# Block attention and feed-forward in one kernel: batch 0's scores from unsplit queries and keys

## The chip, the cores and the metric

The kernel runs on one core of a Trainium2 chip. The metric is the device time of one execution in microseconds, and a version's time is the median of its runs. The engines are called TensorE or PE (matmuls; PEld is its weight load), VectorE or DVE, ScalarE or ACT, GpSimd or POOL, and SyncE or SP, which here issues the DMAs.

## The reference

Inputs are float32: q, k and v of shape (8, 8, 576, 64) (batch, heads, sequence, head dimension) and two weight matrices, w_in (512 x 2048) and w_out (2048 x 512).

```python
scores = (1 / 8) * np.matmul(q, k.transpose(0, 1, 3, 2))
mask = pos[:, None] // 64 >= pos[None, :] // 64        # causal in blocks of 64
scores = np.where(mask, scores, -1e9)
attn = np.exp(scores - max(scores)); attn = attn / (sum(attn) + 1e-9)
x = np.matmul(attn, v)            # (B, H, S, D), then as rows: (B * S, H * D) = (4608, 512)
h = x @ w_in
g = h where h >= 1, 0 where h <= -1, (h + 1) ** 2 / 4 between
out = g @ w_out                   # (4608, 512)
```

## The kernel before

**Words.** The matmuls that need more than one rounded word keep their operands as two: a value is rounded to the type F32R (`hi`), and the remainder (`lo`) is a second F32R value. A product is then two or three matmuls that add up in PSUM. Plain F32 operands can be multiplied too, by one matmul instruction of the source.

**Attention.** There are 32 pairs: 8 batches of 4 pairs of heads, `Pair(b, hp)`. A pair's sequence of 576 is four tiles of 128 and a last block of 64; the last blocks of the two heads share one tile of 128. `SM` is 512, `S` 576, `D` 64 and `P` 128. For a pair, `load_qk` brings q and k in; `split_q` and `split_k` make the two words of each in the tiles `qs` and `ks` (VectorE, and GpSimd for the remainder of k, L353 to L366); `turned(is_q, j)` transposes head j's words on PE (L424), ScalarE copies both words out of PSUM into `qb` or `kb` (L429), and one word of them goes on to `qa` or `ka` by a DMA from SBUF to SBUF (L435; in the very first pair by VectorE for head 0, L431). `turned_last` does the same for the last blocks (L453, L458, L459, without a DMA). `qa` and `ka` hold one word of q and of k in partitions 0 to 63, and four rows more, 64 to 67 (`D` to `KA`), with which the product also adds the mask: the row set is made once in `mrow` at the start (L122 to L138) and copied there by DMA (L150, L151).

`scores(j, g)` makes the scores of head j for a group g of query tiles: group 0 holds tiles 0 and 1 (128 and 256 key columns), group 1 tile 2 (384), group 2 tile 3 (512). `scores_last` takes both heads' last blocks in two halves of 288 columns. Each score product is two matmuls:

```python
nc.tensor.matmul(ps, qa[:KA, j, c0 : c0 + P], ka[:KA, j, k0 : k0 + n], start=first, stop=False)   # L484
nc.tensor.matmul(ps, qb[:, j, c0 : c0 + P], kb[:, j, k0 : k0 + n], start=False, stop=last)        # L487
```

Then VectorE takes the maximum (L508, L533), ScalarE the exponential with its sum (L513, L539), VectorE the scaling (L519, L548). `turn` and `turn_last` transpose the result on PE (L559 or L561) and ScalarE copies it out (L552); `weighted` multiplies by v (L598); L633 and L634 round the result into `xh` and `xl`, the input of the second half.

Batches differ. In batches 0 and 1 (`plain`) the weighted sums are plain F32 matmuls. From batch 2 on (`raw`) q and k are copied first within HBM and split after the transposition.

**Feed-forward.** `ffn_in` (L777) and `ffn_out` (L801, L806) work on chunks of 512 tokens and 128 hidden columns, with two words each. The weights are split into words on the chip, in 32 pieces by `convert` (L165 to L188: a DMA load, ScalarE, VectorE, GpSimd). 

**Order.** A pair is written as eight steps. In the source's order, from step `START` = 36 on, one step of the feed-forward follows each step of attention; 12 of the 32 weight pieces, and two more for the lag, are started within the first 36 steps. The Tile framework orders each engine's instructions when the program is built, by that priority and by readiness, and engines work their queues in order. A tile's buffer is named by its pool and tag; a tag with one buffer gives it to the next tile only when all uses of the tile before are done. `qs` and `ks` have one buffer each, and their tags serve the `raw` batches too. `pa11` is used in batch 1 for a small piece. The loaded `qn` and `kn` share three buffers.

Of the kernel before, what the change touches and what calls it, by code (L numbers as in the profile page):

```python
# [8 lines left out]
F32 = mybir.dt.float32  # L9
# [14 lines left out]
def block_attn_then_ffn(  # L24
# [27 lines left out]
    SCALE = 1.0 / float(D) ** 0.5  # L52
# [4 lines left out]
    KA = D + NTL  # L57
# [2 lines left out]
    FAR = 2  # L60
    RAW = 2
    AT_HOME = 2

    const = ctx.enter_context(tc.tile_pool(name="const", bufs=1))
    att1 = ctx.enter_context(tc.tile_pool(name="att1", bufs=1))
# [12 lines left out]
    def work_bank(name):  # L78

        banks["n"] += 1  # L80
        if banks["free"] and banks["n"] % 2:
            return ps_o.tile([P, 512], F32, tag="po", name=name)
        return ps_w.tile([P, 512], F32, tag="work", name=name)
# [6 lines left out]
    ident = ident_r.bitcast(F32)  # L90
# [11 lines left out]
    qa = const.tile([P, 2, QW], F32R, tag="qa", name="qa")  # L102
    qb = const.tile([P, 2, QW], F32R, tag="qb", name="qb")
    ka = const.tile([P, 2, S], F32R, tag="ka", name="ka")
    kb = const.tile([P, 2, S], F32R, tag="kb", name="kb")

    def last_blocks(t_):

        view = t_[:, :, SM : SM + BLK]
        if t_.shape[2] == S:  # L110
            return view
        part, (_, two), cols = view.ap
        return bass.AP(tensor=view.tensor, offset=view.offset, ap=[part, [QW + BLK, two], cols])


    mrow = att1.tile([NTL, 2, S], F32R, tag="pb0", name="mrow")
# [5 lines left out]
    mtmp = ffn.tile([P, 512], F32, tag="t", name="mtmp")  # L122
# [13 lines left out]
    rows = mrow[:, :, :SM].rearrange("p s (t c) -> p s t c", c=P)  # L136
    nc.vector.tensor_copy(rows[:, 0, :, :BLK], sel)
    nc.vector.tensor_scalar_mul(rows[:, 1, :, BLK:], sel, MASKED)  # L138
    for t_ in (qa, qb):
        nc.vector.tensor_copy(  # L140
            t_[:, :, SM:], mtmp[:, : 2 * (QW - SM)].rearrange("p (h c) -> p h c", h=2)
        )
    for t_ in pcs:
        nc.vector.tensor_copy(t_[BLK:], mtmp[BLK:, : 2 * BLK].rearrange("p (h c) -> p h c", h=2))
    for t_ in vsr:
        nc.vector.tensor_copy(
            t_[BLK:, NTL, :, :], mtmp[BLK:, : 2 * D].rearrange("p (h c) -> p h c", h=2)
        )
    for j in range(2):
        nc.sync.dma_start(qa[D:KA, j, :S].bitcast(F32), mrow[:, 0, :].bitcast(F32))  # L150
        nc.sync.dma_start(ka[D:KA, j, :].bitcast(F32), mrow[:, 1, :].bitcast(F32))  # L151


    shifted = []
# [102 lines left out]
    class Pair:  # L257
# [4 lines left out]
        def __init__(self, b, hp):  # L262
            self.b, self.hp = b, hp

            self.plain = b < PLAIN
            self.first = b == 0 and hp == 0


            self.hop = b >= HOP
            self.raw = b >= RAW  # L270

            self.far = b >= FAR
            self.pr, self.nat = {}, {}

        def fetch(self):
# [68 lines left out]
            self.nat[name] = t_  # L344

        def split_q(self):
            if self.raw:
                return

            qn = self.nat.pop("q")[:, : 2 * NTL + 1, :]  # L350
            self.qs = att1.tile([P, 2 * NTL + 1, 2, D], F32R, tag="qs", name="qs")
            for c0, c1 in ((0, 2 * NTL), (2 * NTL, 2 * NTL + 1)):
                nc.vector.tensor_scalar_mul(self.qs[:, c0:c1, 0, :], qn[:, c0:c1, :], SCALE)  # L353
            nc.vector.scalar_tensor_tensor(
                out=self.qs[:, :, 1, :], in0=qn, scalar=SCALE,
                in1=self.qs[:, :, 0, :].bitcast(F32), op0=ALU.mult, op1=ALU.subtract,
            )

        def split_k(self):
            if self.raw:  # L360
                return
            kn = self.nat.pop("k")[:, : 2 * NTL + 1, :]
            self.ks = att1.tile([P, 2 * NTL + 1, 2, D], F32R, tag="ks", name="ks")
            for c0, c1 in ((0, 2 * NTL), (2 * NTL, 2 * NTL + 1)):
                nc.vector.tensor_copy(self.ks[:, c0:c1, 1, :], kn[:, c0:c1, :])
            (nc.vector if self.first else nc.gpsimd).tensor_tensor(  # L366
                out=self.ks[:, :, 0, :], in0=kn, in1=self.ks[:, :, 1, :].bitcast(F32),
                op=ALU.subtract,
            )
# [29 lines left out]
        def turned_raw(self, j):  # L399
# [10 lines left out]
            for a, bt, hi0 in ((qa, qb, 0), (ka, kb, D)):  # L410
                nc.sync.dma_start(
                    a[:D, j, :SM].bitcast(F32), bt[hi0 : hi0 + D, j, :SM].bitcast(F32)
                )

        def turned(self, is_q, j):

            if self.raw:
                if is_q:
                    self.turned_raw(j)
                return  # L420
            src, a, bt, hi0 = (self.qs, qa, qb, 0) if is_q else (self.ks, ka, kb, D)
            ps = work_bank("ps_qk")
            for t in range(NTL):
                nc.tensor.transpose(  # L424
                    ps[:, t * P : (t + 1) * P].bitcast(F32R), src[:, j * NTL + t, :, :], ident_r
                )

            turned = ps[:, :SM].rearrange("p (t c) -> p c t", t=NTL)
            nc.scalar.copy(bt[:, j, :SM].rearrange("p (c t) -> p c t", t=NTL), turned)  # L429
            if self.first and j == 0:  # L430
                nc.vector.tensor_copy(  # L431
                    a[:D, j, :SM].rearrange("p (c t) -> p c t", t=NTL), turned[hi0 : hi0 + D]
                )
            else:
                nc.sync.dma_start(  # L435
                    a[:D, j, :SM].bitcast(F32), bt[hi0 : hi0 + D, j, :SM].bitcast(F32)
                )

        def turned_last(self):

            ps = work_bank("ps_qk")
            if self.raw:
                ps = ps[:, :P]
                nc.tensor.transpose(ps.bitcast(F32R), self.qk[:, 2 * NTL, :, :], ident_r)
                ps = ps.rearrange("p (h c) -> p h c", h=2)
                self.parted(last_blocks, ps)
                for i, a in enumerate((qa, ka)):
                    nc.vector.tensor_scalar_mul(
                        last_blocks(a)[:D], ps[i * D : (i + 1) * D], 1.0 if i else SCALE
                    )  # L450
                return
            for i, src in enumerate((self.qs, self.ks)):
                nc.tensor.transpose(  # L453
                    ps[:, i * P : (i + 1) * P].bitcast(F32R), src[:, 2 * NTL, :, :], ident_r
                )
            for i, (a, bt, hi0) in enumerate(((qa, qb, 0), (ka, kb, D))):
                blocks = ps[:, i * P : (i + 1) * P].rearrange("p (h c) -> p h c", h=2)
                nc.scalar.copy(last_blocks(bt), blocks)  # L458
                nc.vector.tensor_copy(last_blocks(a)[:D], blocks[hi0 : hi0 + D])  # L459
# [21 lines left out]
                self.x32 = att1.tile([P, S], F32, tag="x32", name="x32")  # L481

        def product(self, ps, j, c0, k0, n, first, last):
            nc.tensor.matmul(  # L484
                ps, qa[:KA, j, c0 : c0 + P], ka[:KA, j, k0 : k0 + n], start=first, stop=False
            )
            nc.tensor.matmul(  # L487
                ps, qb[:, j, c0 : c0 + P], kb[:, j, k0 : k0 + n], start=False, stop=last
            )
# [7 lines left out]
        def scores(self, j, g):  # L497
# [9 lines left out]
            for i, cs in enumerate(cols):  # L507
                nc.vector.tensor_reduce(  # L508
                    out=nm[:, i : i + 1], in_=ps[:, cs], axis=AX.X, op=ALU.max, negate=True
                )  # L510
            raw = ps if self.b < AT_HOME else pr
            for i, cs in enumerate(cols):
# [379 lines left out]
```

## Time and profile before

| What | Value |
|---|---|
| median of 3 runs | 1239.24 us (1237.13 to 1243.8) |
| the profiled execution | 1239.06 us, its span 1237.3 us |
| granted TensorE clock, mean | 0.989 |
| instructions | 19822 |
| DMA | 215.40 MB, mean 174 GB/s |
| first score product (L484) starts | 13.69 us |
| last transposed weights of batch 0 (L561, second head) | about 103 us |

The span is the time from the first to the last instruction on the core. Busy shares are averages over stages that differ: the first 100 us hold batch 0's attention and almost no feed-forward, the last 200 us almost only feed-forward. In the timeline a row is: start, duration, engine, source line, operation, output and inputs, and in brackets the idle time ahead of it with what ended it. In a row of windows the columns are: window, length, then PE, PEld, DVE, ACT and POOL busy with the number of instructions, the granted clock, the DMA share and GB/s. In the chain of work a row is: start, length, engine and line.

### The profile page before, as it was taken

To read this page: it belongs to the slowest core of one execution; us is meant where nothing else is said; L and a number is where in the kernel's file an instruction comes from. 1 tells how busy PE (TensorE), PEld (TensorE's weight loads), DVE (VectorE), ACT (ScalarE), POOL (GpSimd) and SP (SyncE) were. 2 spreads that over 40 slices of the span, in tenths; PEclk is the share of its full clock that TensorE was granted. 3 is DMA by queue.
4 is the path that set the end of the run, shared out by engine and by line. 5 is a ranking of instruction groups with operands and counts; after the bars stand their busy time and mean duration, and the time that the engine had idled before them with its cause. 6 is when DMAs were issued, how large, how long until landed. Compare 5 with 4: busy or idle time off the path is not lost.

```text
span 1237.3 us, 19822 instructions
## 1 busy us (share of the span) xinstructions
PE 1186.6 (96%) x6280; PEld 993.1 (80%) x6280; DVE 863.8 (70%) x2124; ACT 698.5 (56%) x1731; POOL 371.8 (30%) x366
## 2 busy tenths in 40 slices
PE   4878898999999999999999999999999999999998
PEld 3666677788888888888888888888888888888886
DVE  8888778658777877787777877787778776322322
ACT  5877667546566656665666665666566654222222
POOL 3444546312222222222222222222222222222222
PEclk9988998999999999999999999999999999999999
DMA  5756776778986655565555555565556443333332
GB/s 165 213 176 208 235 247 221 225 202 255 291 270 219 192 162 156 147 198 166 163 159 180 164 160 160 148 196 151 155 149 192 142 135 111 119 102 102 120 103 102
DMA packets 177192, 215.40 MB, mean 174 GB/s; under 512 B 109872, under 2 KB 128304, under 8 KB 176320
## 3 DMA queue, kind: packets, MB, share of 16 engines
q1 hardware_dynamic: 177088, 214.14, 56.1%
q8 instruction: 50, 0.82, 0.3%
q14 instruction: 54, 0.44, 0.1%
HBM read 134.74 MB, written 31.98 MB: 135 GB/s over the span
## 4 chain that ended last, share of the span: by engine, by line
PE 86%; DVE 5%; DMA 4%; ACT 2%; issue 2%; POOL 1%; SPq 0%; ACTq 0%; DVEq 0%; POOLq 0%
PE ph L777 31%; PE po L801 20%; PE po L806 10%; PE ps_av L598 9%; PE ps_s L484 5%; PE ps_s L487 4%; PE ps_t L559 4%; PE ps_qk L403 1%; DMA bits<-in_moe_w_in_dram 1%; DVE bits L172 1%; POOL bits L184 1%; PE ps_t L561 1%; DVE nm L508 1%; DVE bits L178 1%; DVE shifted L175 1%
## 5 line engine op out<-in xcount | busy, mean ns | idle before, releaser
L792 POOL TENSOR_TENSOR gl<-t,gh 128x512 fp32r<-128x512 f32 x144 | 186.5, 1295 | 522.8 <-ACT gh L791 338.2
L801 PE MATMUL po<-wo,gh 128*128 128x512 f32 x1152 | 294.1, 396 | 0.1
L801 PEld LDWEIGHTS po<-wo,gh 128*128 128x128 f32 x1152 | 211.2, 188 | 43.3 <-ACT gh L791 0.6
L777 PE MATMUL ph<-xh,wih 128*128 128x512 f32 x576 | 232.7, 404 | 0.4 <-DVE t L790 0.4
L777 PE MATMUL ph<-xh,wil 128*128 128x512 f32 x576 | 228.1, 396 | 0.0
L777 PE MATMUL ph<-xl,wih 128*128 128x512 f32 x576 | 226.9, 394 | 0.0
L787 DVE SCALAR_TENSOR_TENSOR t<-t 128x512 f32<-128x512 f32 x144 | 101.0, 701 | 161.5 <-ACT t L786 158.6
L786 ACT ACTIVATE t<-ph 128x512 f32<-128x512 f32 x144 | 86.2, 599 | 160.5 <-PE ph L777 160.5
L791 ACT CAST gh<-t 128x512 fp32r<-128x512 f32 x144 | 89.4, 621 | 118.9 <-DVE t L790 118.8
L806 PE MATMUL po<-wo,gl 128*128 128x512 f32 x576 | 155.3, 391 | 0.0
L484 PE MATMUL ps_s<-ka,qa 68*128 68x288 f32 (+4 forms) x384 | 133.8, 363 | 4.9 <-DMA ka<-mrow 4.0
L513 ACT ACTIVATE pr<-ps_s,nm 128x128 f32<-128x128 f32 x192 | 100.4, 525 | 57.5 <-DVE nm L508 56.4
L508 DVE TENSOR_REDUCE nm<-ps_s 128x1 f32<-128x128 f32 (+3 forms) x256 | 118.9, 482 | 16.4 <-PE ps_s L487 15.6
L777 PEld LDWEIGHTS ph<-xh,wil 128*128 128x128 f32 x576 | 109.1, 189 | 24.0
L806 PEld LDWEIGHTS po<-wo,gl 128*128 128x128 f32 x576 | 108.0, 188 | 22.9
L777 PEld LDWEIGHTS ph<-xl,wih 128*128 128x128 f32 x576 | 109.6, 190 | 19.3
L777 PEld LDWEIGHTS ph<-xh,wih 128*128 128x128 f32 x576 | 109.2, 190 | 19.3 <-DVE t L790 0.8
L381 POOL TENSOR_TENSOR vsr<-vn,vsr 64x64 fp32r<-64x64 f32 (+1 forms) x96 | 56.5, 589 | 227.1 <-ACT vsr L380 226.0
L487 PE MATMUL ps_s<-kb,qb 128*128 128x288 f32 (+4 forms) x384 | 120.4, 321 | 0.0
L790 DVE TENSOR_TENSOR t<-ph,t 128x512 f32<-128x512 f32 x144 | 98.7, 685 | 2.0
L559 PEld LDWEIGHTS ps_t<-ident_r,prr 128*128 128x128 f32 x600 | 68.5, 139 | 22.4 <-issue 0.5
L494 DVE TENSOR_SCALAR sm<-sm 128x1 f32<-128x1 f32 x256 | 38.5, 151 | 65.0 <-ACT pr L513 54.8
(115 smaller groups left out, 1879.7 us busy)
## 6 DMA issues: line engine op xcount, KB each, us to landing
wo<-wo_split SPq DMA_DIRECT2D x144, 512.0 KB, 3.4
prr<-pr SPq DMA_DIRECT2D x96, 192.0 KB, 3.0
prr<-pr SPq DMA_DIRECT2D x48, 256.0 KB, 2.8
out_dram<-ob SPq DMA_DIRECT2D x36, 256.0 KB, 2.9
bits<-in_moe_w_in_dram SPq DMA_DIRECT2D x16, 512.0 KB, 4.6
bits<-in_moe_w_out_dram SPq DMA_DIRECT2D x16, 512.0 KB, 4.0
wo_split<-ws SPq DMA_DIRECT2D x16, 512.0 KB, 2.9
qa<-qb SPq DMA_DIRECT2D x63, 128.0 KB, 2.4
```

The costliest lines, as they stand in the source:

```text
L484: nc.tensor.matmul(ps, qa[:KA, j, c0 : c0 + P], ka[:KA, j, k0 : k0 + n], start=first, stop=False)
L487: nc.tensor.matmul(ps, qb[:, j, c0 : c0 + P], kb[:, j, k0 : k0 + n], start=False, stop=last)
L508: nc.vector.tensor_reduce(out=nm[:, i : i + 1], in_=ps[:, cs], axis=AX.X, op=ALU.max, negate=True)
L513: nc.scalar.activation(raw[:, cs], ps[:, cs], AF.Exp, bias=nm[:, i : i + 1], scale=1.0, accum_out=sm[:, i : i + 1],)
L559: nc.tensor.transpose(out.bitcast(F32R), src, ident_r)
L598: nc.tensor.matmul(ps[:, lo_col:], vt, x, start=first and i == 0 and m == 0, stop=last and i == len(parts) - 1 and m == len(mov) - 1,)
L777: nc.tensor.matmul(ph, w[:, cc, fs], x[:, cc, xs], start=(cc == 0 and i == 0), stop=(cc == NCC - 1 and i == 2),)
L787: nc.vector.scalar_tensor_tensor(out=t_, in0=t_, scalar=1.0, in1=t_, op0=ALU.min, op1=ALU.mult)
L790: nc.vector.tensor_tensor(out=t_, in0=ph, in1=t_, op=ALU.max)
L792: nc.gpsimd.tensor_tensor(out=gl, in0=t_, in1=gh.bitcast(F32), op=ALU.subtract)
L801: nc.tensor.matmul(po[tt], gh[:, ts_], wo[:, w, :], start=(fc == 0 and w == 0), stop=False)
L806: nc.tensor.matmul(po[tt], gl[:, ts_], wo[:, 0, :], start=False, stop=fc == NFC - 1)
```

## The change

In batch 0 (`WHOLE` = 1) q and k are not split. `turned_whole` transposes the loaded F32 tiles (64 columns wide instead of the 128 of two words), and ScalarE copies the result, with the scale for q, straight into `qw` or `kw`; there is no second copy by DMA. The last blocks of q go into a tile of their own, `ql`. A score product is one F32 matmul. `qw` and `kw` use the buffers of the tags `qs` and `ks`, `ql` that of `pa11`. The mask's rows are copied into `qw` and `kw` as well (four DMAs more, ahead of those into `qa` and `ka`), and `ql` is cleared at the start. Batches 1 to 7 are as before.

```diff
+    WHOLE = 1
...
+    qw = att1.tile([P, 2, SM], F32, tag="qs", name="qw")
+    ql = att1.tile([P, 2, P], F32, tag="pa11", name="ql")
+    kw = att1.tile([P, 2, S], F32, tag="ks", name="kw")
...
+    nc.vector.tensor_copy(ql, mtmp[:, : 2 * P].rearrange("p (h c) -> p h c", h=2))
...
-    for j in range(2):
-        nc.sync.dma_start(qa[D:KA, j, :S].bitcast(F32), mrow[:, 0, :].bitcast(F32))
-        nc.sync.dma_start(ka[D:KA, j, :].bitcast(F32), mrow[:, 1, :].bitcast(F32))
+    for a, b in ((qw, kw), (qa, ka)):
+        n = min(S, a.shape[2])
+        for j in range(2):
+            nc.sync.dma_start(a[D:KA, j, :n].bitcast(F32), mrow[:, 0, :n].bitcast(F32))
+            nc.sync.dma_start(b[D:KA, j, :].bitcast(F32), mrow[:, 1, :].bitcast(F32))
...
         def split_q(self):
-            if self.raw:
+            if self.raw or self.whole:
                 return
...
         def split_k(self):
-            if self.raw:
+            if self.raw or self.whole:
                 return
...
+        def turned_whole(self, is_q, j):
+
+            src, dst = (self.nat["q"], qw) if is_q else (self.nat["k"], kw)
+            ps = work_bank("ps_qk")[:D]
+            for t in range(NTL):
+                nc.tensor.transpose(ps[:, t * P : (t + 1) * P], src[:, j * NTL + t, :], ident)
+            nc.scalar.mul(
+                dst[:D, j, :SM].rearrange("p (c t) -> p c t", t=NTL),
+                ps[:, :SM].rearrange("p (t c) -> p c t", t=NTL),
+                SCALE if is_q else 1.0,
+            )
...
         def turned_last(self):
             ps = work_bank("ps_qk")
+            if self.whole:
+                for i, (name, dst) in enumerate((("q", ql), ("k", kw))):
+                    cols = ps[:D, i * P : (i + 1) * P]
+                    nc.tensor.transpose(cols, self.nat.pop(name)[:, 2 * NTL, :], ident)
+                    nc.scalar.mul(
+                        last_blocks(dst)[:D],
+                        cols.rearrange("p (h c) -> p h c", h=2),
+                        1.0 if i else SCALE,
+                    )
+                return
...
         def product(self, ps, j, c0, k0, n, first, last):
+            if self.whole:
+                tile_q = ql[:KA, j, :] if c0 == SM else qw[:KA, j, c0 : c0 + P]
+                nc.tensor.matmul(
+                    ps, tile_q, kw[:KA, j, k0 : k0 + n], start=first, stop=last
+                )
+                return
```

`last_blocks`, the view of a tile's last-block columns, is made general so that it fits `ql` and `kw` too.

More of the change, by code (lines that the diff above doesn't have):

```diff
@@ L105, in block_attn_then_ffn @@
     kb = const.tile([P, 2, S], F32R, tag="kb", name="kb")
+    qw = att1.tile([P, 2, SM], F32, tag="qs", name="qw")
+    ql = att1.tile([P, 2, P], F32, tag="pa11", name="ql")
+    kw = att1.tile([P, 2, S], F32, tag="ks", name="kw")
     def last_blocks(t_):
-        view = t_[:, :, SM : SM + BLK]
+        at = max(0, min(SM, t_.shape[2] - 2 * BLK))
+        view = t_[:, :, at : at + BLK]
         if t_.shape[2] == S:
-            return view
+            return t_[:, :, SM:]
         part, (_, two), cols = view.ap
-        return bass.AP(tensor=view.tensor, offset=view.offset, ap=[part, [QW + BLK, two], cols])
+        step = t_.shape[2] + BLK
+        return bass.AP(tensor=view.tensor, offset=view.offset, ap=[part, [step, two], cols])
     mrow = att1.tile([NTL, 2, S], F32R, tag="pb0", name="mrow")
@@ L272, in __init__ @@
             self.far = b >= FAR
+            self.whole = b < WHOLE
             self.pr, self.nat = {}, {}
@@ L413, in turned_raw @@
                 )
+        def turned_whole(self, is_q, j):
[8 more added lines that the diff above has]
+            )
         def turned(self, is_q, j):
+            if self.whole:
+                return self.turned_whole(is_q, j)
             if self.raw:
@@ L483, in product @@
         def product(self, ps, j, c0, k0, n, first, last):
+            if self.whole:
+                tile_q = ql[:KA, j, :] if c0 == SM else qw[:KA, j, c0 : c0 + P]
[3 more added lines that the diff above has]
+                return
             nc.tensor.matmul(
```

## The prediction

> **What bounds the kernel now.** I read the page first, for the engines and the chain of work that ended last.
>
> ```profile
> span 1237.3 us, 19822 instructions
> ...
> PE 1186.6 (96%) x6280; PEld 993.1 (80%) x6280; DVE 863.8 (70%) x2124; ACT 698.5 (56%) x1731; POOL 371.8 (30%) x366
> ...
> PE 86%; DVE 5%; DMA 4%; ACT 2%; issue 2%; POOL 1%; SPq 0%; ACTq 0%; DVEq 0%; POOLq 0%
> ```
>
> Over the whole span TensorE is the bound: the chain lies on PE for 86%. But the change touches batch 0 alone, so I cut the span into stretches. The first product starts at 13.69 us; the last of batch 0's products ends at 98.64.
>
> ```profile
> 0.00:13.60 13.60, 2.52 (x18) 2.33 (x18) 9.25 (x26) 4.80 (x8) 1.78 (x10) 1.00 0.63 168
> 13.60:110.00 96.40, 75.59 (x402) 61.34 (x403) 84.87 (x243) 74.74 (x196) 46.03 (x42) 0.93 0.64 197
> 110.00:200.00 90.00, 79.71 (x386) 62.63 (x384) 67.57 (x151) 57.98 (x134) 44.23 (x39) 0.92 0.71 227
> ```
>
> The columns after the length are PE, PEld, DVE, ACT and POOL busy. From 13.6 to 110 us VectorE is the fullest: 84.87 of 96.40 us, 88%. PE shows 75.59, and ScalarE 74.74. So batch 0 is held by VectorE first, with ScalarE close behind, and PE has some room; from batch 1 on PE is fullest. Nothing waits for a fixed time later, so what batch 0 gains or loses moves all that follows.
>
> **What it takes off VectorE.** These are the groups of that stretch that go, in part.
>
> ```profile
> L366 POOL TENSOR_TENSOR ks<-kn,ks 128x576 fp32r<-128x576 f32 x5 | 7.2, 1440 | 6.4 <-PE ps_av L598 3.8 <-DMA rawk<-in_k_dram 2.1 <-DVE sm L495 0.2
> ...
> L354 DVE SCALAR_TENSOR_TENSOR qs<-qn,qs 128x576 fp32r<-128x576 f32 x5 | 3.7, 748 | 0.0
> ...
> L353 DVE TENSOR_SCALAR qs<-qn 128x512 fp32r<-128x512 f32 x5 | 2.3, 458 | 0.0
> L365 DVE CAST ks<-kn 128x512 fp32r<-128x512 f32 x5 | 2.1, 416 | 0.0
> ...
> L365 DVE CAST ks<-kn 128x64 fp32r<-128x64 f32 x5 | 1.8, 353 | 0.0
> ...
> L459 DVE CAST ka<-ps_qk 64x128 fp32r<-64x128 f32 x5 | 1.5, 294 | 0.2
> ...
> L459 DVE CAST qa<-ps_qk 64x128 fp32r<-64x128 f32 x5 | 1.4, 271 | 0.0
> L353 DVE TENSOR_SCALAR qs<-qn 128x64 fp32r<-128x64 f32 x5 | 0.9, 184 | 0.0
> ```
>
> Of the five splittings in the stretch three belong to pairs 1 to 3 of batch 0; the other two are batch 1's and stay. Of the five turns of the last blocks four are batch 0's. VectorE loses 3/5 of 2.3 + 0.9 + 3.7 + 2.1 + 1.8 = 6.5 us, and 4/5 of 2.9 = 2.3 us: 8.8 us. GpSimd loses 3/5 of 7.2 = 4.3 us. Some of the VectorE time is not on the chain. The one large removed piece that is on it is a hop by DMA from kb to ka:
>
> ```profile
> 8.71 4.84 DMA ka<-mrow
> ...
> 13.69 0.45 PE ps_s L484
> ...
> 53.14 2.37 DMA ka<-kb
> ...
> 98.21 0.43 PE ps_s L487
> ```
>
> So the gain lies between 2.4 us (only that hop) and 8.8 us (every freed VectorE microsecond). I take 8.8, because an engine that is 88% busy and works its queue in order is nearest to that end. Fourteen such hops go (two in pair 0, four in each later pair), and their issues leave SP's queue. ScalarE keeps its copies out of PSUM: the same 512 columns, from 64 partitions, with the scale folded in. I put that at nothing. The transposes stay 18 a pair, each still a matmul record against the identity: nothing.
>
> **What it puts on TensorE.** The two rounded products of a tile become one 32-bit product. A 32-bit product is already in the trace: the attention-times-value matmuls of batches 0 and 1.
>
> ```profile
> 15.32 0.63 PE L484 MATMUL ps_s<-ka,qa 68*128 68x512 f32 x1
> 15.74 0.63 PE L487 MATMUL ps_s<-kb,qb 128*128 128x512 f32 x1
> ...
> 103.70 2.17 PE L598 MATMUL ps_av<-pb,vs 128*128 128x320 f32 x8
> 105.80 0.43 PE L598 MATMUL ps_av<-pc,vs 64*128 64x64 f32 x2
> ...
> 108.66 0.50 PE L484 MATMUL ps_s<-ka,qa 68*128 68x512 f32 x1
> ...
> 109.23 0.30 PE L484 MATMUL ps_s<-ka,qa 68*128 68x288 f32 x1
> ...
> 109.77 0.40 PE L777 MATMUL ph<-xh,wih 128*128 128x512 f32 x1
> ```
>
> Ends are modelled, so I take starts. The eight records from 103.70 to 105.80 are four 32-bit products (each leaves two records) of 320, 320, 320 and 192 columns: 2.10 us for 1152 columns, 1.82 ns a column. The two-word products: 512 columns from 108.66 to 109.23, 1.11 ns a column, and two of 288 from 109.23 to 109.77, 0.94; the mean is 1.03. The ratio is 1.82 / 1.03 = 1.77. A pair has 2 x (128 + 256 + 384 + 512) + 4 x 288 = 3712 columns of scores, so PE gets 3712 x 0.79 ns = 2.9 us more in each of four pairs, 11.7 us. In pair 0 the 512 columns of one word take 0.42 us (15.32 to 15.74), about twice as long as later although the granted clock of that stretch reads 1.00, so there it is nearer 5.8 us, and the whole 14.6 us.
>
> How much of it lies on the path? On the chain between 13.69 and 98.64 stand 16 pieces of L484 and L487 (the first and the last are quoted above), 5.04 us together. At 1.77 they grow by 3.9 us. Bounds: none, if PE's idle time takes it all, and 14.6. I take the chain's 3.9.
>
> The Trainium skill, FP8 and Floating Point Precision, section TensorE Precision Notes, says that true 32-bit products take four passes through the array. Against the two products of the present form that would be an estimated ratio of 2.0 instead of the rows' 1.77, and the chain's pieces would grow by 5.0 us instead of 3.9; the forecast would be 1234.3.
>
> **The start.** Now the mask's rows are made late, behind the splitting of the first pair, and their copies queue behind two loads of weights.
>
> ```profile
> 3.09 0.36 DVE L146 CAST vsr<-mtmp 64x128 fp32r<-64x128 f32 x2
> ...
> 3.96 0.48 DVE L125 MEMSET msel<- 4x512 f32 x1
> ...
> 4.51 0.41 POOL L126 TENSOR_SCALAR_AFFINE_SELECT msel<-msel 4x256 f32<-4x256 f32 x1 [2.95 <-DVE qs L353]
> ...
> 6.16 0.76 DVE L366 TENSOR_TENSOR ks<-kn,ks 128x576 fp32r<-128x576 f32 x1
> 6.66 1.06 SPq L165 DMA_DIRECT2D bits<-in_moe_w_in_dram  x2
> ...
> 6.97 0.27 DVE L137 CAST mrow<-msel 4x256 fp32r<-4x256 f32 x1
> ...
> 7.18 0.28 DVE L138 TENSOR_SCALAR mrow<-msel 4x256 fp32r<-4x256 f32 x1
> ...
> DMA to landing us min/median/max: 2.2/2.6/5.9
> ```
>
> Without the splits VectorE clears msel after L146 and the new zeroing of ql (about 0.3 us, an estimate from L146): from 3.75 to 4.25. GpSimd's select ends near 4.75, and L137 and L138 near 5.3 instead of 7.46. The copies are then issued before the weight loads of 6.66, and should land in about the 2.2 us that the last row (the hops of L435) has as its least, not the 4.84 that the chain shows for ka<-mrow. That is 2.1 + 2.6 = 4.7 us less at most, and nothing if the loads still go first. There are eight copies instead of four, but the whole tiles' four go first. The first products also need q and k turned, which by then they are. I take 4.0.
>
> **The boundary to batch 1.** qw and kw sit in the slots of qs and ks (one buffer each). Batch 1's first split can be written only when pair 3's last product has read qw and kw; now it needs only pair 3's transposes.
>
> ```profile
> 98.01 0.63 PE L487 MATMUL ps_s<-kb,qb 128*128 128x512 f32 x1
> ...
> 101.92 0.29 PE L484 MATMUL ps_s<-ka,qa 68*128 68x128 f32 x1
> ```
>
> From 98.64 on come, by the means above, the splitting of q (0.46 + 0.18 + 0.75), k's rounding (0.42 + 0.35) and GpSimd's rest (1.44), four transposes and a copy (about 1.0, an estimate), and a hop (2.4): about 7.0 us, so 105.6 instead of 101.92, 3.7 us later. Queued behind it are pair 4's reductions on VectorE and its exponentials on ScalarE; PE can meanwhile do pair 3's weighted sums, which take from 103.70 to 108.66. Bounds: 0, if these cover it, and 3.7 + 2.1 if VectorE's queue delays the split as well. I take 3.0. The raw loads qn and kn are held longer, until the last blocks are turned; three buffers and some half a pair of time cover that, and without the cover it would cost one load's landing.
>
> **Sum.** -4.0 - 8.8 + 3.9 + 3.0 = -5.9 us. The profiled execution took 1239.06 us, its span 1237.3 and 1.8 around it; it lies 0.2 below the median of 1239.24. Forecast: 1233.2 us.
>
> **Rivals.**
>
> - The freed VectorE time is hidden anyway. ScalarE's 74.74 us speak for it: with VectorE at 76 the two are level, and weight conversion passes through both. Then only the hop counts: -4.0 - 2.4 + 3.9 + 3.0 = +0.5, 1239.6 us.
> - GpSimd's removed work frees VectorE more than its own rows say. For it speaks the spread of one and the same operation:
>
> ```profile
> L172 DVE TENSOR_SCALAR bits<-bits x32: 409/430/1657, 11.8 to 217.5; 128x512 f32<-128x512 f32 x32
> ```
>
>   Least, median and largest are 409, 430 and 1657 ns: it is held up by something, and GpSimd works in that stretch. If each removed GpSimd microsecond held VectorE, 4.3 us more go: 1228.9 us. The Trainium skill, SBUF — State Buffer, section SBUF: two separate sides, says that VectorE and GpSimd share a pair of ports that one instruction locks wholly. By that rule this is what would happen; the row's spread agrees, but doesn't name the holder.
> - Slower: PE becomes batch 0's bound. Its records leave 20.8 us of 96.40 idle, with 14.6 us to come. If that idle time is only there because results arrive late, each product's delay is passed on through reduction, exponential and turn, and all 14.6 us count: +14.6 - 2.4 - 4.0 + 3.0 = +11.2, 1250.3 us. It decides once more than 3.4 us of stretched products lie on the path (2.4 + 4.0 - 3.0) while VectorE's gain stays at the hop.
>
> That the change doesn't do what it says can be only in part: the 32-bit product is one instruction in the source and two records on PE.
>
> **How the numbers follow.** Forecast 0.46 (its own range 1230 to 1237), hidden 0.21, more freed 0.20, slower 0.13. Within 0.5% (6.2 us, about what a measurement can tell here) means 1233.0 to 1245.4. The forecast's case lies on both sides of 1233.0: I give 0.25 of it to faster and 0.21 to the same. Faster: 0.25 + 0.20 = 0.45. Same: 0.21 + 0.21 = 0.42, and 0.01 of the slower case. Slower: 0.12. The range for 8 in 10 reaches from 1226, the case of more freed with a covered boundary, to 1243, which leaves out the slower case's upper part.
>
> **What would show it.** Right: the first product near 9.7 us; VectorE's busy time between the first product and pair 3's last smaller by about 9 us; two records for each score product, at 1.8 ns a column; batch 1's first split just after pair 3's last product, with PE on weighted sums meanwhile. Wrong: a first product still after 13 us, PE without idle time in batch 0, or a VectorE that is less busy while the stretch is as long as before.

## The result and the profile after

The changed kernel takes 1251.4 us (median of 5 runs, 1247.91 to 1252.61) against 1239.24 before: a ratio of 1.0092, 95% interval 1.0068 to 1.0115. It is 12.2 us slower, where 1233.2 was forecast, and it lies above the range of 1226 to 1243; slower had been given a chance of 0.12. The profiled execution took 1250.88 us.

The head of the page:

```profile
span 1248.8 us, 19750 instructions
...
PE 1202.0 (96%) x6280; PEld 997.5 (80%) x6280; DVE 854.0 (68%) x2094; ACT 697.3 (56%) x1731; POOL 368.4 (30%) x363
```

VectorE shows 9.8 us less (863.8 before), PE 15.4 us more (1186.6). To see where that counts I cut both traces at the same three events: batch 0's first score product, the end of its last, batch 1's first, and the start of the 15th `t<-ph` on ScalarE, from when on the difference between the kernels moves by less than 1 us. First before, then after:

```profile
13.69:98.64 84.95, 64.23 (x342) 52.06 (x343) 74.50 (x211) 66.36 (x175) 41.12 (x37) 0.93 0.62 189
98.64:101.92 3.28, 3.28 (x18) 2.86 (x18) 3.21 (x9) 2.58 (x7) 0.82 (x2) 0.66 0.87 250
101.92:255.50 153.58, 141.08 (x708) 112.20 (x708) 113.79 (x260) 98.35 (x232) 71.63 (x65) 0.96 0.72 227
```

```profile
13.74:99.27 85.53, 73.26 (x330) 51.38 (x330) 68.98 (x185) 64.78 (x172) 34.98 (x34) 0.88 0.62 197
99.27:109.31 10.04, 6.46 (x34) 5.76 (x35) 5.31 (x16) 5.45 (x13) 2.65 (x2) 0.69 0.64 212
109.31:266.20 156.89, 142.91 (x704) 114.10 (x704) 113.21 (x257) 95.40 (x229) 72.45 (x63) 0.93 0.69 217
```

Read the lengths: the start is where it was (13.69, 13.74); batch 0's stretch is 85.53 instead of 84.95 us although VectorE works 5.5 us less in it; the gap to batch 1 grows from 3.28 to 10.04, and batch 1 up to that event from 153.58 to 156.89. So +0.05 + 0.58 + 6.76 + 3.31 = +10.7 us of the 11.5 by which the spans differ, most of it in one gap in which no score product runs. The gap in the timeline of after:

```profile
98.25 1.02 PE L521 MATMUL ps_s<-kw,qw 68*128 68x512 f32 x2
...
99.31 0.53 DVE L364 TENSOR_SCALAR qs<-qn 128x512 fp32r<-128x512 f32 x2
...
100.09 0.75 DVE L365 SCALAR_TENSOR_TENSOR qs<-qn,qs 128x576 fp32r<-128x576 f32 x1
...
100.89 0.54 PE L449 MATMUL ps_qk<-ident_r,qs 128*128 128x128 f32 x4 [1.62 <-DVE qs L365]
101.14 1.30 POOL L198 TENSOR_TENSOR ws<-bits,ws 128x512 fp32r<-128x512 f32 x1 [5.27 <-ACT ws L196]
...
102.39 1.40 POOL L377 TENSOR_TENSOR ks<-kn,ks 128x576 fp32r<-128x576 f32 x1
...
103.85 0.75 PE L449 MATMUL ps_qk<-ident_r,ks 128*128 128x128 f32 x4 [1.95 <-POOL ks L377]
...
105.25 0.49 SPq L460 DMA_DIRECT2D ka<-kb  x1
...
109.31 0.43 PE L525 MATMUL ps_s<-ka,qa 68*128 68x128 f32 x1
```

The last product of batch 0 ends at 99.27; the first split of batch 1 (L364) begins at 99.31. Behind it stand in series the rest of q's split, the turn, k's remainder on GpSimd (which first finishes a weight piece, L198), the turn of k and the hop to `ka`. In the kernel before, these splits were made while pair 3 still multiplied: GpSimd's remainder ran at 85.41 there. The end of the gap is PE's own queue: from 106 to 110 us PE has no idle time, while its granted clock reads 0.51 (1.00 in the same window of e9 below); in the 8 us ahead PE was busy for 4.28.

### The profile page after: what moved, and what is told of

Read it like the earlier page. It is cut to its first block, busy times and chain, and to the rows that moved or that the text cites. A ratio compares the mean times of both kernels' runs of the same rounds, so it can differ in the third digit from the quotient of the medians.

```text
span 1248.8 us, 19750 instructions
## 1 busy us (share of the span) xinstructions
PE 1202.0 (96%) x6280; PEld 997.5 (80%) x6280; DVE 854.0 (68%) x2094; ACT 697.3 (56%) x1731; POOL 368.4 (30%) x363
## 4 chain that ended last, share of the span: by engine, by line
PE 80%; DVE 2%; ACT 1%; DMA 0%; issue 0%; ACTq 0%; SPq 0%; DVEq 0%
PE ph L818 29%; PE po L842 20%; PE po L847 10%; PE ps_av L639 8%; PE ps_s L525 5%; PE ps_t L600 4%; PE ps_s L528 4%; PE ps_qk L414 1%; PE ps_qk L479 0%; DMA vsr<-pr 0%; DVE bits L188 0%; DVE t L828 0%; DVE t L831 0%; DVE nm L549 0%; ACT t L827 0%
## 5 line engine op out<-in xcount | busy, mean ns | idle before, releaser
L525 PE MATMUL ps_s<-ka,qa 68*128 68x128 f32 (+1 forms) x336 | 115.1, 358 | 2.7 <-ACT pa L593 2.6
L528 PE MATMUL ps_s<-kb,qb 128*128 128x128 f32 (+1 forms) x336 | 103.7, 316 | 0.0
```

## Experiments

Ratios are to the kernel before, on the same chip. "First" is the start of batch 0's first score product, "stretch" from there to the end of its last, "gap" from there to batch 1's first. All times are us; the kernel before took 1239.17 to 1239.63 on the chips of the experiments.

| Kernel | time | ratio (95%) | first | stretch | gap |
|---|---|---|---|---|---|
| before | 1239.24 | | 13.69 | 84.95 | 3.28 |
| after | 1251.4 | 1.0092 (1.0068 to 1.0115) | 13.74 | 85.53 | 10.04 |
| e1_own_slots | 1240.53 | 1.0013 (0.9996 to 1.003) | 13.55 | 83.2 | 2.5 |
| e2_mask_act | 1253.46 | 1.0112 (1.0098 to 1.0127) | 18.12 | 88.0 | 8.3 |
| e3_one_word | 1237.84 | 0.9983 (0.9972 to 0.9994) | 13.96 | 76.4 | 7.5 |
| e4_before_mask_act | 1248.49 | 1.0074 (1.0062 to 1.0086) | 17.47 | 92.1 | 3.3 |
| e5_own2 | 1245.33 | 1.0044 (1.0028 to 1.006) | 11.86 | 92.5 | 2.4 |
| e6_own2_splits | 1243.17 | 1.0027 (1.0017 to 1.0037) | 11.85 | 92.5 | 2.4 |
| e7_own2_mask_pool | 1238.89 | 0.9998 (0.9989 to 1.0007) | 12.04 | 86.5 | 2.4 |
| e8_v_moved | 1247.21 | 1.0059 (1.0044 to 1.0074) | 11.58 | 89.0 | 8.3 |
| e9_clean | 1235.77 | 0.9973 (0.9965 to 0.9982) | 13.68 | 85.7 | 3.0 |
| e10_clean_mask_pool | 1242.45 | 1.0029 (1.0015 to 1.0043) | 8.71 | 90.3 | 3.5 |
| e11_before_mask_pool | 1243.4 | 1.0034 (1.0023 to 1.0045) | 15.19 | 83.5 | 5.9 |
| e12_before_late_split | 1251.13 | 1.0105 (1.0086 to 1.0124) | 13.42 | 85.6 | 10.3 |
| e13_clean_one_word | 1237.6 | 0.9984 (0.9972 to 0.9995) | 13.65 | 79.3 | 3.2 |
| e14_clean_splits | 1253.3 | 1.0113 (1.0093 to 1.0132) | 13.70 | 93.4 | 2.5 |

Behind the gap, from batch 1's first product to the 15th `t<-ph`, it took 153.58 us in before, 156.89 in after, 156.72 in e1, 156.61 in e3, 155.50 in e6, 147.41 in e9, 158.18 in e12, 158.12 in e13 and 158.10 in e14.

### The shared slots: e1, e12, e9

Theory: `qw` and `kw` in the buffers of `qs` and `ks` make batch 1's first split wait for batch 0's last product, and that wait is the loss. Rival: the longer products are the loss, and the gap only shows it. e1 gives `qw` and `kw` other buffers.

```diff
-    qw = att1.tile([P, 2, SM], F32, tag="qs", name="qw")
-    kw = att1.tile([P, 2, S], F32, tag="ks", name="kw")
+    qw = [ffn.tile([P, SM], F32, tag=t_, name="qw") for t_ in ("gh", "gl")]
+    vq = att1.tile([P, 2 * 2 * (NTL + 1) * D + 2 * S], F32, tag="pb1", name="vq")
...
+    kw = vq[:, 4 * (NTL + 1) * D :].rearrange("p (j s) -> p j s", j=2)
```

> The changed kernel, but qw and kw lie in buffers that batch 1's qs and ks don't use (qw in the feed-forward's gh and gl, kw beside the values in pb1). Theory S (the shared slots): batch 1's first split no longer waits for pair 3's last product, the gap from that product's end to batch 1's first product falls from 10.0 us to 3 to 4, as before the change, and the time from 1251.4 to 1242 to 1245. Rival P (the 32-bit products and the slow clock hold TensorE up there): the gap stays over 8 us and the time at 1248 to 1253.

The gap closed to 2.5 and 10.9 us came back, as theory S says. But k shares a persistent tile with the values there, and the second part of the weighted sums of batches 0 and 1 used the next pair's values, since their load was not held back. So it is a hint, not a price.

e12 asks from the other side. It is the kernel before, with nothing of the change but the delay: two one-column additions on VectorE, behind batch 0's last product, read the last pair's split words, so that their buffers come free only then.

```diff
+            if self.b == 0 and self.hp == NPAIR - 1 and (j, g) == (1, 2):
+                for x in (self.qs, self.ks):
+                    nc.vector.tensor_tensor(
+                        out=sm[:, 1:2], in0=nm[:, :1], in1=x[:, 0, 0, :1].bitcast(F32), op=ALU.add
+                    )
```

> The kernel before, all its products and splits as they were, but pair 3's words of q and k are kept until its last product: two VectorE additions of one column (0.15 us each), which read them and that product's maximum, hold their buffers. So batch 1's first split waits as in the changed kernel. Theory S: the gap at the boundary grows from 3.3 to 8 to 10 us and the time from 1239.5 to 1245 to 1250. Rival (the gap is there because of the 32-bit products): gap under 5 us, time within 2 us of 1239.5.

1251.13 us: with two-word products, all splits and all hops in place, the delay alone costs about what the whole change costs (1.0105 and 1.0092 of before), more than theory S's 1245 to 1250. 7.05 us of it stand in the gap and 4.6 in batch 1. Its windows around the boundary, and from its timeline the addition, the split it holds, and the first product:

```profile
13.42:98.99 85.57, 65.73 (x329) 52.47 (x329) 73.22 (x208) 65.69 (x173) 40.72 (x37) 0.84 0.66 202
98.99:109.32 10.33, 6.63 (x35) 5.80 (x35) 7.73 (x17) 5.37 (x11) 4.37 (x4) 0.54 0.41 132
```

```profile
100.81 0.15 DVE L513 TENSOR_TENSOR sm<-nm,qs 128x1 f32<-128x1 f32 x1
...
100.99 1.63 DVE L353 TENSOR_SCALAR qs<-qn 128x512 fp32r<-128x512 f32 x2
...
109.32 0.29 PE L484 MATMUL ps_s<-ka,qa 68*128 68x128 f32 x1
```

The split starts 1.7 us later than in after (100.99, 99.31), since the addition waits its turn on VectorE; the first product starts at the same time (109.32, 109.31).

e9 is the clean version of e1: the change whole, with the values as they were. `qw` and `kw` take the buffers of `gh` and `gl`, which the feed-forward uses later, and the last blocks of k go beside those of q. A product over the last blocks' columns becomes two (224 and 64 columns).

```diff
-    qw = att1.tile([P, 2, SM], F32, tag="qs", name="qw")
-    ql = att1.tile([P, 2, P], F32, tag="pa11", name="ql")
-    kw = att1.tile([P, 2, S], F32, tag="ks", name="kw")
+    qw = [ffn.tile([P, SM], F32, tag=t_, name="qw") for t_ in ("gh", "gl")]
+    kw = [ffn.tile([P, SM], F32, tag=t_, name="kw") for t_ in ("gh", "gl")]
+    lasts = att1.tile([P, 3 * P], F32, tag="pa11", name="lasts")
```

> The changed kernel with the values loaded where they were, and only qw and kw in other buffers: both in the feed-forward's gh and gl, k's last blocks beside ql in pa11; so the second half of the last blocks' product is two products (224 and 64 columns, eight matmuls more a pair, about 0.8 us). Theory S: the gap at the boundary falls from 10.0 to 2 to 4 us, batch 0's stretch stays at 85 to 88, the time is 1241 to 1246. Rival: the gap was not what the time hung on, and what is won there is lost in batch 1: 1249 or more.

```profile
13.68:99.35 85.67, 75.72 (x360) 54.67 (x361) 72.18 (x193) 64.87 (x175) 36.78 (x35) 0.87 0.62 193
99.35:102.39 3.04, 2.71 (x22) 2.36 (x21) 2.33 (x6) 3.04 (x8) 1.30 (x1) 1.00 0.67 217
102.39:249.80 147.41, 135.65 (x705) 109.08 (x705) 113.71 (x259) 95.88 (x230) 70.68 (x63) 0.99 0.73 234
```

Start and stretch are those of after, the gap is gone (GpSimd's remainder for batch 1 runs at 84.74), and 15.6 us come back: 1235.77 us, below before and after. That is less than theory S's 1241 to 1246.

The shared slots are shown as the cause of the gap from both sides: taken out (e1, e9), it closes; put alone into the kernel before (e12), it opens. The times go with it, by 10.9, 15.6 and 11.9 us, which is more than the gap's 7. That more is not shown to be the slots': 9.5 of e9's 15.6 us come in batch 1, but e13 and e14 have no such gap either, and their batch 1 is as long as e12's. Nor is e9's lead over before shown to be a gain of the change: all of it lies in batch 1 (147.41 against 153.58), where the two kernels have the same source.

### The start: e2, e4, e7, e10, e11

The forecast let the mask's rows land 4 us earlier. In after they are made early but not sent early:

```profile
5.20 0.27 DVE L145 TENSOR_SCALAR mrow<-msel 4x256 fp32r<-4x256 f32 x1
...
6.65 1.06 SPq L175 DMA_DIRECT2D bits<-in_moe_w_in_dram  x2
...
7.83 0.76 SPq L160 DMA_DIRECT2D qw<-mrow  x1
...
8.70 0.63 SPq L161 DMA_DIRECT2D kw<-mrow  x1
```

`mrow` is ready at 5.47; SP issues its copies at 7.83, behind loads of v and the two weight loads of 6.65, as before. The trace of after puts the wait of its first product down to a ScalarE row (L180) that ends at 13.70, those of before and e9 to the copy of the mask's rows. e2 (after) and e4 (before) issue them from ScalarE's queue, e11 (before), e10 (e9) and e7 (e5, below) from GpSimd's. The edit, with `nc.gpsimd` in the latter three:

```diff
-            nc.sync.dma_start(a[D:KA, j, :n].bitcast(F32), mrow[:, 0, :n].bitcast(F32))
-            nc.sync.dma_start(b[D:KA, j, :].bitcast(F32), mrow[:, 1, :].bitcast(F32))
+            nc.scalar.dma_start(a[D:KA, j, :n].bitcast(F32), mrow[:, 0, :n].bitcast(F32))
+            nc.scalar.dma_start(b[D:KA, j, :].bitcast(F32), mrow[:, 1, :].bitcast(F32))
```

> The changed kernel, but the eight copies of the mask's rows are issued from ScalarE's queue, not from SP's behind the loads of v and of the weights. If that order alone kept the start from shrinking: first product near 9.5 us instead of 13.74, the time 4 us less, 1247. Rival: the copies land no earlier, or the 4 us are lost again to the weight pieces that ScalarE and VectorE then start no earlier: 1250 to 1253.

> The kernel before, with its four copies of the mask's rows issued from ScalarE's queue. If the start's wait belongs to the order on SP's queue and not to the change: first product near 10.5 us instead of 13.69 (its rows are made 2 us later than in the changed kernel), the time 1236. Rival: no earlier product, 1239.

Both miss: the first product comes 4 us later, not earlier. e4's ScalarE waits for the rows, issues four copies, and only then loads its table and empties PSUM (11.76). On VectorE a split of pair 1 (L353) has come to stand ahead of the copies into `qa` and `ka` (L431), and waits for its load until 15.67; the first product waits for those copies until 17.47:

```profile
7.34 1.17 ACTq L150 DMA_DIRECT2D qa<-mrow  x1
...
10.47 1.28 ACT L429 ACT_TABLE_LOAD   x1 [10.47 <-DMA qa<-mrow]
...
15.67 0.43 DVE L353 TENSOR_SCALAR qs<-qn 128x512 fp32r<-128x512 f32 x1 [8.16 <-DMA qn<-in_q_dram]
```

> The same kernel, with the mask's rows copied from GpSimd's queue, which has nothing to do then, instead of SP's. If the place behind the weight loads is what the first product waits for: first product at 8 to 10 us instead of 13.6, and since later work is held by engines' queues, the time 3 to 4 us less, about 1237. If the DMA engines themselves are full of the weights: first product still after 12 us, no change.

> The kernel before, with its four copies of the mask's rows from GpSimd's queue. If the start's wait is the queue order and independent of the change: first product 2 to 3 us earlier than 13.69, the time 1236 to 1238. If the order of the rest matters more than the start: 1239 to 1243.

> The same, with the mask's rows copied from GpSimd's queue. If the copies' place behind the loads of v and of the weights is the start's price: first product at 9 to 11 us instead of 13.7, the time 3 to 4 us less than without. If the two words in which the gain of the like run came (its stretch was 6 us shorter, its first product not earlier) are an accident of the order: within 3 us of the run without, to either side.

e10 answers the question on the start for e9's order. The first product comes at 8.71, 5 us earlier than in e9, so there the copies' place in SP's queue was what it waited for; and yet the kernel is slower (1242.45 against 1235.77), which neither forecast had. Its timeline behind the start:

```profile
8.71 2.40 PE L527 MATMUL ps_s<-kw,qw 68*128 68x128 f32 x8 [0.71 <-DMA kw<-mrow]
...
11.79 0.65 ACT L185 ACTIVATE bits<-bits 128x512 f32<-128x512 f32 x1 [3.23 <-DMA bits<-in_moe_w_in_dram]
...
12.90 0.33 ACT L563 ACTIVATE ps_s<-ps_s,nm 128x128 f32<-128x128 f32 x1
...
15.69 0.42 PE L475 MATMUL ps_qk<-ident_r,kn 128*64 128x128 f32 x1 [4.58 <-ACT lasts L476]
```

ScalarE's queue holds a weight conversion (L185) ahead of the exponentials, and that waits for its load until 11.79; the exponentials start at 12.90, the last blocks' copy follows them, and PE waits 4.58 us for it. Pair 1's first product starts at 35.81, in e9 at 34.40. The gain was turned into a new wait, for a load of weights. In e11 GpSimd issues the copy half a microsecond earlier than SP did before (8.20, 8.71), and the product that waits for it starts 1.5 us later (15.19, 13.69):

```profile
8.20 0.52 POOL L151 DMA_DIRECT2D ka<-mrow  x1
...
15.19 0.45 PE L484 MATMUL ps_s<-ka,qa 68*128 68x128 f32 x1 [5.60 <-DMA ka<-mrow]
```

So the time of landing isn't the time of issue and a constant: from issue to product it is 7.0 us here, 5.0 before, and 2.4 in e10, where the copy goes out at 6.35. In e10 itself the four copies of L166 took from 2.2 to 6.8 us to land. e7's first product comes no earlier than e5's (12.04, 11.86), and yet it is 6.4 us faster, by a shorter stretch; why the stretch is shorter I can't say.

### Values loaded later: e5, e6, e8

e5 keeps e1's tile and loads the values of batches 0 and 1 behind the older pair's last weighted sums, so that each pair has its own; e8 is after with that move alone; e6 is e5 with batch 0's splitting put back on VectorE and GpSimd, read by nobody.

```diff
-                cur.load("v")
+                if not cur.plain:
+                    cur.load("v")
...
+            if cur and cur.plain:
+                cur.load("v")
```

> The changed kernel with qw and kw in buffers of their own, as in the first experiment, but with a pair's values loaded only behind the older pair's last weighted sums in the source's order (in the first experiment the second part of the weighted sums of batches 0 and 1 used the next pair's values, and so the load didn't wait for them). Theory S: gap between batch 0's last product and batch 1's first one 3 to 4 us, time 1239 to 1243. If the first experiment's 11 us came from the load that didn't wait: gap over 6 us or a longer stretch, time 1246 or more.

> Control: the changed kernel with its shared slots, and only the load of the values moved behind the older pair's last weighted sums in the source's order. If theory S holds: gap still 9 to 11 us, time 1249 to 1253. If the place of this load made the difference: 1243 or less.

> The same kernel, with batch 0's splitting of q and k put back as in the kernel before (three VectorE operations for q, two and one of GpSimd for k, in their old places), its results read by nobody: 12 us of VectorE work, 3.9 of it before the first product. If VectorE is what holds batch 0: the stretch from the first to the last product 7 to 9 us longer than without, the time 7 to 12 us more. If TensorE's longer products hold it: 0 to 3 us more.

e5's gap is closed, but its stretch is 92.5 us, so it can't price the slots. e8 misses both its forecasts (gap 8.3, 1247.21): with the moved load alone the first product comes 2.2 us earlier than in after (11.58) and batch 0's last ends 1.3 us later (100.61). The windows of e5 and then e6:

```profile
11.86:104.33 92.47, 80.68 (x344) 56.30 (x345) 71.95 (x189) 66.05 (x176) 35.01 (x34) 0.94 0.58 182
```

```profile
11.85:104.36 92.51, 78.17 (x344) 55.40 (x345) 74.39 (x201) 65.36 (x173) 38.26 (x36) 0.82 0.58 184
```

The splitting is back and the stretch is the same: in this order VectorE's freed time is worth nothing. The last two runs say otherwise for e9's order.

### Products and VectorE apart: e3, e13, e14

e3 is after with the tiles of q and k as one rounded word (F32R in place of F32): the remainders are left out, the products become short, and the shared slots stay. e13 is the same edit on e9, without the slots' wait. e14 is e9 with the splitting put back, read by nobody.

```diff
-    qw = att1.tile([P, 2, SM], F32, tag="qs", name="qw")
+    qw = att1.tile([P, 2, SM], F32R, tag="qs", name="qw")
```

> The changed kernel, but qw, ql and kw are of the rounded type, so that a score product is one product of one rounded word (the remainders are left out of the result). It keeps everything else, the shared slots too. TensorE gets some 1.3 ns a column less for 14848 columns, about 19 us in batch 0. Theory P: the stretch from the first to the last product of batch 0 falls from 85.5 us to below 79, the time by 7 us or more, below 1244. Theory S: most of the loss is the boundary, which stays at 10 us; the stretch falls by 0 to 4 us, the time is 1247 to 1251.

> The kernel with queries and keys of batch 0 turned into slots of other tiles (35.77 us above 1200 before), but turned and multiplied as one rounded word: the remainders are left out, the transposes and the copies stay where they are. It prices the longer 32-bit products alone, since the wait at the boundary is gone. Theory A (the products lie on batch 0's chain, so their price was set too low in the forecast): first to last product of batch 0 falls from 85.7 us to 76 to 79, and the time by 6 to 9 us, to about 1228. Theory B (VectorE's copies and masks pace batch 0, the products are covered): the stretch stays at 84 to 86 and the time at 1234 to 1237.

> The same kernel with 32-bit products and its own slots, and the splitting of batch 0 put back on VectorE and GpSimd: its results are read by nobody. It prices the freed VectorE time alone. Theory A (VectorE's time was on batch 0's chain, worth the 8.8 us of the forecast, and the products ate it): the stretch grows from 85.7 us to 92 to 95 and the time by 6 to 9 us, to about 1243. Theory B (VectorE's time was never on the chain): the stretch stays within 85 to 88 us and the time at 1235 to 1238. The wait of batch 1's split on the slots comes back with the shared buffers only as far as these writes are late: a gap at the boundary above 4 us would be told apart from the stretch.

The windows of e13, then of e14:

```profile
13.65:92.94 79.29, 62.07 (x303) 49.23 (x304) 65.04 (x188) 64.38 (x172) 34.50 (x33) 0.76 0.63 200
...
96.18:254.30 158.12, 139.69 (x704) 112.08 (x704) 119.82 (x265) 99.35 (x235) 73.65 (x66) 0.96 0.70 218
```

```profile
13.70:107.05 93.35, 79.29 (x360) 57.53 (x361) 76.58 (x206) 65.35 (x174) 41.50 (x37) 0.84 0.61 191
...
109.50:267.60 158.10, 139.75 (x704) 111.16 (x704) 118.20 (x263) 97.24 (x232) 71.53 (x64) 0.97 0.70 220
```

With e9's 85.67 these give both prices within the stretch. e14 has the splitting, and it costs 93.35 - 85.67 = 7.7 us, GpSimd's part included. e14 against before (both split; e14 with 32-bit products, and turned without hops and without the casts of L459) costs 93.35 - 84.95 = 8.4 us, which is the price of the longer products less what the missing hops and casts gave. The two cancel in e9; both are taken through the same run e14, so their sum is no further evidence. One rounded word instead of 32 bits saves 85.67 - 79.29 = 6.4 us, and in e3, which is theory P's case, 85.53 - 76.42 = 9.1 us. So by the stretch theory A holds in e14 and nearly in e13 (76 to 79 was forecast): VectorE's time was on the chain, and the products took its place. Each stretch is one profiled execution, so a microsecond either way is not to be read.

The times follow less well: theory A gave about 1228 for e13 and 1243 for e14. e13 reaches batch 1 6.2 us before e9 and ends later than it; e3, with a stretch of 76.4, is at 1237.84. Batch 1 up to the same event took 158.12 us in e13, 147.41 in e9, 153.58 before: the same work in another order, and at another granted clock (0.96, 0.99, 0.96). Why the order of e9 is that good and that of e13 that bad stays open, and so does the part of e14's loss that comes behind its stretch.

## Why the prediction was wrong, point by point

**The terms.** Up to batch 1's first product the forecast was -5.9 us and the trace has +7.4 (109.31 - 101.92). Each term beside what it measured:

| Term | forecast | measured | from |
|---|---|---|---|
| start | -4.0 | 0.05 | first product 13.74 instead of 13.69 |
| freed VectorE time | -8.8 | -7.7 | e9 against e14 (splits alone) |
| longer products | +3.9 | +8.4 | e14 against before (hops and casts gone too) |
| boundary | +3.0 | +6.8 | gap 10.04 instead of 3.28 |
| batch 1 | nothing | +3.3 | 156.89 instead of 153.58 |

**Start: the step "the copies are then issued before the weight loads of 6.66" failed.** The rows were early as forecast (5.47, estimate 5.3), but on SP's queue the loads kept their place. The 0 of the bounds was right. And e10 shows that in e9's order the term was wrong a second time: even with the rows there at 8.71, the next wait ends at 11.79 and nothing is left of the gain.

**VectorE: about right in size, in part by luck.** Of the 8.8 us the splits were 6.5 and the casts of L459 2.3; the 7.7 measured are the splits with GpSimd's remainder, without the casts. What PE's transposes of the weights waited for on VectorE in batch 0's stretch, before and then after (time in total, number, longest):

```profile
PE ps_t L561 <- DVE pr L519: 9.7, 6, 3.2
PE ps_t L561 <- DVE sm L494: 6.9, 3, 2.9
```

```profile
PE ps_t L602 <- DVE pr L560: 5.1, 4, 2.3
PE ps_t L602 <- DVE sm L535: 1.8, 2, 1.6
PE ps_t L602 <- DVE sm L536: 1.5, 1, 1.5
```

16.6 us of waits became 8.4. That is not the freed time alone: the same waits are 13.6 us in e14 with the splits, 8.9 in e9 without them, but 16.2 in e13, which has no splits either and short products. So the longer products hide a part of VectorE's time too. And the 7.7 hold for e9's order alone (e6 against e5: nothing).

**Products: the step "I take the chain's 3.9" failed.** PE's time on score products in the stretch, before and after:

```profile
13.69:98.64 84.95, 25.62 (x96) 0.93 0.62 189
```

```profile
13.74:99.27 85.53, 35.86 (x96) 0.88 0.62 197
```

They grew by 10.2 us (11.7 to 14.6 forecast), and e14 puts what counted at 8.4. The price of a column was about right, the share on the path was not. Pair 3's products over the last blocks, with the transposes that follow them, before and after:

```profile
86.10 0.37 PE L484 MATMUL ps_s<-ka,qa 68*128 68x288 f32 x1
...
87.25 0.49 PE L561 MATMUL ps_t<-ident_r,pr 128*128 128x128 f32 x3
```

```profile
92.19 2.11 PE L521 MATMUL ps_s<-kw,ql 68*128 68x288 f32 x8
94.13 0.49 PE L602 MATMUL ps_t<-ident_r,pr 128*128 128x128 f32 x3
```

By the starts 1152 columns take 1.94 us instead of 1.15, a ratio of 1.69 (1.77 forecast). The pieces on the chain before are a lower bound: once VectorE's waits go, PE's own time is what stands between them. In after PE is busy for 73.26 of 85.53 us, VectorE for 68.98. The other way less counts: e13 has 19.1 us less of product time than e9 (18.08, 37.19) and is 6.4 us shorter. The slower rival named this mechanism, but it counted all 14.6 us and left VectorE's gain at the hop. That its 1250.3 lies near 1251.4 is luck: e9, with the same products, is at 1235.77.

The estimated ratio of 2.0 by the Trainium skill (FP8 and Floating Point Precision, TensorE Precision Notes) is not what these rows show: 1.69 from starts, and 35.86 / 25.62 = 1.40 in busy time, in which modelled ends overlap.

**Boundary: the mechanism was named, the size was not.** The slots' wait came as described, and was 6.8 us where 3.0 was taken and 5.8 was the bound. The step that failed is that pair 3's weighted sums would cover it. PE is busy for 6.46 of the 10.04 us; they came in the gap, but the chain of splits did not get shorter by it. The bound had left out GpSimd's piece of weights ahead of k's remainder (1.25 us, from 101.14 to 102.39) and the second head's turns ahead of the first product. It had no clock in it either: the granted clock is 0.69 in after's gap and 0.54 in e12's, 1.00 in e9's and 0.66 in the short one of before. Of the 6.46 us an estimated 2 us are due to that (6.46 x 0.69 = 4.5). Nor did the forecast let it grow, for batch 1 stood in no term: 7.4 us at batch 1's first product are 10.7 at the event and 11.5 in the span. Why stays open. e12 goes from 7.4 to 12.0 us likewise, but so does e14, whose gap is 2.5 (7.6 to 12.1).

**The other rivals.** That freed VectorE time is hidden is refuted for e9's order by e14. More freed is not borne out: VectorE fell by 5.5 us in the stretch, less than the 8.8 of the rows removed. The operation it was argued from and its neighbour, here before and after:

```profile
L172 DVE TENSOR_SCALAR bits<-bits 128x512 f32<-128x512 f32 x14 | 11.2, 801 | 3.1 <-ACT bits L170 3.1
L178 DVE SCALAR_TENSOR_TENSOR bits<-bits,shifted 128x512 uint32<-128x512 uint32 x13 | 9.0, 694 | 0.1
```

```profile
L188 DVE SCALAR_TENSOR_TENSOR bits<-bits,shifted 128x512 uint32<-128x512 uint32 x15 | 12.9, 858 | 0.2
...
L182 DVE TENSOR_SCALAR bits<-bits 128x512 f32<-128x512 f32 x14 | 9.2, 654 | 2.6 <-issue 1.4 <-ACT bits L180 1.1
```

The first (L172, L182 after) did get shorter, from 801 to 654 ns, in the direction of the Trainium skill's rule (SBUF — State Buffer, SBUF: two separate sides). The second (L178, L188) got longer, from 694 to 858 ns, and took back what the first gave. No run here shows what held either.

**The range** of 1226 to 1243 would have held e9, but by the short batch 1 of its order. No single term made the 18.2 us between forecast and result: the start is 4.0 of them, the products 4.5, the boundary 3.8, batch 1, which had no term, 3.3, VectorE 1.1. The bounds that the terms themselves were given add up to 0 - 2.4 + 14.6 + 5.8 = +18.0 us, well above 1243; the range had left out their upper part. The boundary passed even its bound, which was summed from rows of single operations without what stands in the queues between them.

## What to carry to other kernels

A new tile that borrows a buffer's tag carries the release time of its last reader into everything that uses the tag next: before costing the operations of a change, ask for each shared buffer when it came free before, when it comes free now, and how long the series behind it is. Where two engines are nearly level in a stretch, the pieces that happen to lie on today's chain are only a lower bound for what is put on one of them: here 3.9 us lay on the chain, 10.2 us were added and 8.4 counted. And a start made earlier is worth only the distance to the next thing that is late there.

## What the runs showed of the hardware that I had not expected

- A copy of 8 or 9 KB within SBUF took 2.4 to 7.0 us from issue to the product that waits for it (e10, before, e11), and four like copies in one kernel took 2.2 to 6.8 us to land (e10, L166).
- Four small DMA issues on ScalarE's queue held its first copy out of PSUM until 11.76 us, since the wait for the rows, the issues (7.34 to 10.43) and the table load of 1.28 us stand in one queue (e4).
- After 8 us in which TensorE was busy for 4.28, its granted clock read 0.51 from 106 to 110 us, in which it was busy throughout (after); in e9, busy for 7.67 of the same 8 us, it read 1.00 throughout.
- Batch 1 up to the same event, with the same source, took from 147.41 (e9) to 158.18 us (e12), in other orders and at granted clocks of 0.93 to 0.99 (0.93 in after, 0.99 in e9, 0.96 in e12 and e13). No run parts order and clock. The spread is as large as the effect under study, so a gain of a few microseconds ahead of it can't be read from the total alone.
